# An attention and two-product kernel: blocks eight and nine share the first product, as seven products of full width

## The chip, the cores and the metric

The kernel runs on one core of one Trainium2 chip. The metric is the device time of one execution in microseconds (us). The engines are TensorE (PE for its matmuls, PEld for its weight loads), VectorE (DVE), ScalarE (ACT), GpSimd (POOL) and SyncE (SP, which here only issues DMAs).

## The reference, cut to what matters

```python
q, k, v: (8, 8, 576, 64)     # batch, heads, sequence, head width; all float32
q_s = exp(q - max(q, -1));  q_s /= sum(q_s, -1) + 1e-9
k_s = exp(k - max(k, 2));   k_s /= sum(k_s, 2) + 1e-9
kv  = einsum('bhsd,bhse->bhde', k_s, v)
x   = einsum('bhsd,bhde->bhse', q_s, kv)   # -> (4608 tokens, 512)
h   = x @ w_in                             # (4608, 512) @ (512, 2048): the first large product
g   = s * relu(h) ** 2 + b
out = g @ w_out                            # (4608, 2048) @ (2048, 512): the second large product
```

## The kernel before, in words

**Blocks and steps.** The 4608 tokens are cut into nine blocks of 512. Blocks one to eight (numbers 0 to 7 in the code) hold the first 512 tokens of each of the eight batches; block nine (number 8) holds the 64 tokens that each batch has left over. A block takes 16 steps, one for each 128 of the 2048 middle columns; step t is block t // 16, column group f = t % 16, and there are 144 steps. The weights are converted once, during block one, and stay in SBUF: `wi[f]` and `wo[f]` lie in the tile `wt[f]`.

**Three matmuls for each product.** Every operand is kept as a high and a low part (`xh`, `xl`; `w[:, 0]`, `w[:, 1]`; `gh`, `gl`) of the type float32r, and high by high, high by low and low by high are summed. So `h_parts` issues 12 matmuls of 128x512 for one step (four chunks of 128 of the 512 inputs, three matmuls each), and `o_parts` 12 more (four tiles of 128 tokens). Between them ACT makes `r = relu(h)`, DVE squares and scales it, ACT adds b and rounds it to `gh`, DVE computes `gl`. On the PE the order is h of step t, then the second product of step t - 1.

**Ahead of a block** its x is made from q, k and v (k maxima, exponentials, `kv`, `xp`), pair of heads by pair of heads. The input tiles `k0`, `q0` and `v0` are tiles of their own, filled again for each pair by SP's queue: `load_v` issues four head loads and then one for the left-over rows. The left-over 64 tokens of a pair go through a DRAM tensor, `xleft`, by `keep_left` and `store_left`; `left_over` brings all of them back as block nine's x, and ACT and POOL split it into its two parts, one chunk every second step.

**What sets the order.** Every piece of work is an `Op`: an engine, a planned cost, a due time, what it needs, takes, frees and gives. The class `Order` plays these on paper and fixes, for each engine, the order in which its instructions stand; on the chip each engine runs its own list in order and waits only for the data hazards of the tiles. The planner's costs are not times of the chip.

**The end.** The last step of block nine is cut into halves to shorten its chain, and `leave_last` copies four result tiles and stores each by two DMAs.

Of the kernel before, what the change touches and what calls it, by code (L numbers as in the profile page):

```python
# [8 lines left out]
F32 = mybir.dt.float32  # L9
F32R = mybir.dt.float32r  # L10
# [3 lines left out]
AF = mybir.ActivationFunctionType  # L14
# [12 lines left out]
def attention_moe(ctx: ExitStack, tc: tile.TileContext, q, k, v, w_in, w_out, s, b, out):  # L27
# [7 lines left out]
    NQ = 4  # L35
# [27 lines left out]
    kvfs = [const.tile([P, 2, 2, D], F32, name=f"kvf{i}") for i in range(2)]  # L63

    early = work.tile([P, 2 * NT * P], F32, name="early", tag="qhl")
    for t in kvfs:
        nc.gpsimd.memset(t, 0.0)
    sb = const.tile([P, 2], F32, name="sb")
# [7 lines left out]
    second = xpool.tile([P, 2 * NP * TB], F32, name="raw1", tag="x")  # L76
    raws = [
        (const.tile([P, KQ], F32, name="k0"), const.tile([P, KQ], F32, name="q0"), const.tile([P, VW], F32, name="v0")),
# [157 lines left out]
    def keep_left(u, x):  # L236
        pr, i = divmod(u, 2)
        if pr not in xl_:
            xl_[pr] = work.tile([P, 2, LEFT], F32, name=f"xleft_{pr}", tag="xleft", bufs=2), set()
        t, there = xl_[pr]  # L240
        nc.scalar.copy(t[:, i], x)
        there.add(i)
        if len(there) == 2 and pr < NP:
            store_left(pr)
# [207 lines left out]
    def k_tiles(pr):  # L452
        m2 = work.tile([P, 4, 2, D], F32, name=f"m2_{pr}", tag="m2")
        m1 = work.tile([P, 4, D], F32, name=f"m1_{pr}", tag="m1")
        return m2, m1, small.tile([P, 2], F32, name=f"km_{pr}", tag="km")
# [46 lines left out]
    def k_tops(pr, m):  # L502
        top = small.tile([P, 4, 2], F32, name=f"top_{pr}", tag="top", bufs=1)
# [194 lines left out]

    def left_over():

        due = NSTEP - 2 * NFC
        yield Op(
            "SP", 0.65, due, needs=[f"left{pr}" for pr in range(NP, NU // 2)] + [f"h{due - 1}"], take=["w"], kb=1024, gives=["left"]
        )
        xf = wpool.tile([P, NP, TB], F32, name="xleft_all", tag="w")
        nc.sync.dma_start(xf, xleft)
        xh, xl = x_tile(B)
        for c in range(NP):
            yield Op("ACT", 0.55, due + 2 * c, needs=["left"] + [f"h{due + 2 * c}"])
            nc.scalar.copy(xh[:, c], xf[:, c])  # L710
            yield Op("POOL", 1.1, due + 2 * c, gives=[f"x{B * NP + c}"])
            nc.gpsimd.tensor_tensor(out=xl[:, c], in0=xf[:, c], in1=xh[:, c].bitcast(F32), op=ALU.subtract)
# [25 lines left out]
    def step(t):  # L738
# [10 lines left out]
        yield Op("ACT", 0.5, t - 2, take=["r", "g"], free=["h"] if t < NSTEP - 1 else ())  # L749
        r, gh, gl = g_tiles(t)  # L750
        if t == NSTEP - 1:

            halves = [slice(i * TB // 2, (i + 1) * TB // 2) for i in range(2)]
            for i, c in enumerate(halves):
                if i:
                    yield Op("ACT", 0.35, t - 2, free=["h"])
                nc.scalar.activation(r[:, c], hp_[:, c], AF.Relu)
            for c in halves:
                yield Op("DVE", 0.4, t - 2)
                nc.vector.scalar_tensor_tensor(out=r[:, c], in0=r[:, c], scalar=s_col, in1=r[:, c], op0=ALU.mult, op1=ALU.mult)  # L760
            for c in halves:
                yield Op("ACT", 0.4, t - 2)
                nc.scalar.activation(gh[:, c], r[:, c], AF.Identity, bias=b_col)
            for i, c in enumerate(halves):
                yield Op("DVE", 0.4, t - 2, free=["r"] if i else (), gives=[f"g{t}"] if i else ())
                nc.vector.scalar_tensor_tensor(
                    out=gl[:, c], in0=r[:, c], scalar=b_col, in1=gh[:, c].bitcast(F32), op0=ALU.add, op1=ALU.subtract
                )
        else:
            nc.scalar.activation(r, hp_, AF.Relu)  # L770
        if t == NSTEP - 1:
            pass
        elif first and (t % 2):
# [19 lines left out]
        for i, j in enumerate(tile_order(t)):  # L793
# [6 lines left out]
    def tile_order(t):  # L800

        return (0, 2, 1, 3) if t == NSTEP - 1 else range(NQ)

    def o_parts(t):
# [4 lines left out]
        for j in tile_order(t):  # L809
# [22 lines left out]
    def leave_last(j):  # L832

        t = NSTEP - 1

        yield Op("DVE" if j == 2 else "ACT", 0.6, t, needs=[f"o{t} {j}"])
        if not lasts:
            lasts.append(work.tile([P, 2 * NT * P], F32, name="last", tag="qhl"))
        o = work.tile([P, DO], F32, name=f"o_{B}_{j}", tag="qe", bufs=2) if j > 1 else lasts[0][:, j * DO:(j + 1) * DO]
        (nc.vector.tensor_copy if j == 2 else nc.scalar.copy)(o, acc[B, j // 2][:, j % 2])  # L840
# [6 lines left out]
    NU = B * NP  # L847
    NBLK = B + 1
# [27 lines left out]
    def others():  # L876
# [8 lines left out]
        one = small.tile([P, 1], F32, name="one", tag="one", bufs=1)  # L885
# [43 lines left out]
    def idle(us, last):  # L929
# [7 lines left out]
        "maxima": 2, "turned": 2, "xleft": 2, "tmp": NTMP, "w": NFC + 1  # L937
# [3 lines left out]
    with tc.manual_schedule(engines={E.PE, E.DVE, E.Activation, E.Pool, E.SP}):  # L941
# [42 lines left out]
```

## Time and profile before

| | |
|---|---|
| median of 3 timed runs | 872.81 us (871.5 to 873.91) |
| profiled execution, first to last instruction | 869.5 us |
| PE busy | 851.7 us, 98% |
| DVE, ACT, POOL busy | 570.8, 416.3, 91.4 us |
| matmuls of the first product | 1728 of 128x512 |
| matmuls of the second product | 1728 of 128x512 |

The profile gives the profiled execution as a span; its own time on the device is not listed apart. The median of the runs lies 3.3 us above that span (872.81 - 869.5), which is taken for what lies around it. In the profile a row of a timeline has a start, a duration, an engine, a line of the kernel, the operation with its tiles, and a count; "[idle before <-releaser]" says how long the engine had been idle and which instruction ended that. In a row that groups instructions, the numbers after the bar are busy time and the mean duration in nanoseconds.

### The profile page before, as it was taken

The page shows a single profiled execution, that of the slowest core. Times are in us where ns is not written, and L with a number is a line of the kernel's source. Part 1 is how long each engine was busy: PE and PEld are TensorE (multiplying, and loading weights), DVE is VectorE, ACT ScalarE, POOL GpSimd, SP SyncE. Part 2 cuts the span into 40 slices and gives each one's busy share as a digit, 9 for nine tenths or more (in the row PEclk, how much of TensorE's full clock was granted, in tenths as well). Part 3 has the DMA queues.
Part 4 walks back from the last instruction along what each step waited for, and adds up shares of the span by engine and source line. Part 5 has one row for each costly group of instructions (what it writes and reads, how often), then busy time and mean ns, then how long its engine had stood idle before and what let it go on. Part 6 is the DMA issues. An engine that isn't in the chain of part 4 may idle for free.

```text
span 869.5 us, 11637 instructions
## 1 busy us (share of the span) xinstructions
PE 851.7 (98%) x4367; PEld 701.9 (81%) x4367; DVE 570.8 (66%) x916; ACT 416.3 (48%) x694; POOL 91.4 (11%) x117
## 2 busy tenths in 40 slices
PE   7799999999999999999999999999999999999997
PEld 6578887888888888888888888888888888888886
DVE  6999997596877777686677658785855322232222
ACT  5989864544554545353545354444544322222222
POOL 1000002021102111111021202020200010000000
PEclk9999999999999999999999999999999999999999
DMA  8994134424433334342433242432311000000001
GB/s 232 308 378 136 26 86 118 127 74 97 137 82 89 83 119 100 90 92 78 130 89 83 89 130 75 96 89 82 77 61 52 33 16 1 1 30 19 1 1 48
DMA packets 109991, 79.44 MB, mean 91 GB/s; under 512 B 60656, under 2 KB 103664, under 8 KB 109808
## 3 DMA queue, kind: packets, MB, share of 16 engines
q1 hardware_dynamic: 108496, 77.60, 31.8%
q10 hardware_dynamic: 1440, 1.12, 0.4%
q8 instruction: 34, 0.56, 0.3%
q14 instruction: 21, 0.17, 0.1%
HBM read 60.29 MB, written 18.40 MB: 91 GB/s over the span
## 4 chain that ended last, share of the span: by engine, by line
PE 92%; DVE 4%; DMA 1%; SPq 1%; issue 1%; ACT 0%; ACTq 0%; DVEq 0%
PE acc L814 44%; PE h L726 44%; PE kv L299 2%; PE xp L676 1%; PE xq L676 1%; DMA k<-in_k_dram 1%; DVE low L216 1%; DMA st<-in_moe_w_in_dram 0%; DVE st L213 0%; PE xp L440 0%; DVE w L223 0%; DMA v<-in_v_dram 0%; SPq L288 0%; DVE low L206 0%; DVE st L211 0%
## 5 line engine op out<-in xcount | busy, mean ns | idle before, releaser
L726 PE MATMUL h<-x,w 128*128 128x512 f32 x1728 | 420.2, 391 | 2.4 <-ACT r L770 1.2
L726 PEld LDWEIGHTS h<-x,w 128*128 128x128 f32 x1728 | 322.7, 188 | 71.6 <-ACT r L770 1.9
L814 PE MATMUL acc<-w,gh 128*128 128x512 f32 x1152 | 357.8, 392 | 0.8 <-ACT gh L780 0.8
L814 PEld LDWEIGHTS acc<-w,gh 128*128 128x128 f32 x1152 | 214.0, 188 | 45.6 <-ACT gh L780 1.2
L785 DVE SCALAR_TENSOR_TENSOR r<-r,sb 128x512 f32<-128x512 f32 x135 | 106.1, 786 | 190.1 <-ACT r L770 189.7
L814 PE MATMUL acc<-w,gl 128*128 128x512 f32 x576 | 224.5, 390 | 0.6 <-DVE gl L782 0.6
L770 ACT ACTIVATE r<-h 128x512 f32<-128x512 f32 x143 | 85.5, 598 | 277.3 <-PE h L726 264.9
L789 DVE SCALAR_TENSOR_TENSOR gl<-r,sb,gh 128x512 fp32r<-128x512 f32 x135 | 104.5, 774 | 56.5 <-ACT gh L787 55.2
L787 ACT ACTIVATE gh<-r,sb 128x512 fp32r<-128x512 f32 x135 | 97.7, 724 | 84.8 <-DVE r L785 84.4
L814 PEld LDWEIGHTS acc<-w,gl 128*128 128x128 f32 x576 | 108.1, 188 | 23.8 <-DVE gl L782 1.1
L575 POOL TENSOR_TENSOR q<-q,qm 128x640 f32<-128x640 f32 x24 | 33.7, 1406 | 161.4 <-DVE qm L573 161.4
L592 POOL TENSOR_TENSOR qe<-qe,qr 128x640 f32<-128x640 f32 x24 | 32.3, 1347 | 65.8 <-DVE qr L588 43.7
L682 ACT COPY y<-xp 64x320 f32<-64x320 f32 x48 | 20.2, 420 | 13.8 <-PE xp L676 13.4
L686 DVE TENSOR_TENSOR y<-xp,y 64x320 f32<-64x320 f32 x48 | 23.5, 489 | 3.4 <-ACT y L682 2.5
L562 ACT ACTIVATE k<-k 128x640 f32<-128x640 f32 x24 | 17.7, 737 | 15.1 <-DVE k L524 12.3
L596 DVE STREAM_TRANSPOSE q<-qe 128x640 f32<-128x640 f32 x24 | 19.9, 831 | 5.2 <-POOL qe L592 5.2
L299 PEld LDWEIGHTS kv<-v,k 128*64 128x64 f32 x600 | 18.7, 137 | 5.1 <-issue 4.4
L656 POOL TENSOR_TENSOR spare<-kvf,spare 128x256 fp32r<-128x256 f32 x12 | 10.1, 844 | 118.6 <-issue 112.8
L613 DVE TENSOR_TENSOR qhl<-qT,qhl 64x640 fp32r<-64x640 f32 x24 | 20.6, 860 | 1.1 <-ACT qhl L610 0.4
L686 DVE TENSOR_TENSOR y<-xq,y 64x256 f32<-64x256 f32 x48 | 20.3, 422 | 1.0
L299 PE MATMUL kv<-v,k 128*64 128x65 f32 (+1 forms) x600 | 20.8, 224 | 0.0
L200 ACT ACTIVATE low<-st 128x1024 int32<-128x1024 uint32 (+1 forms) x17 | 18.9, 1111 | 3.2 <-DVE w L223 1.9
(124 smaller groups left out, 619.6 us busy)
## 6 DMA issues: line engine op xcount, KB each, us to landing
st<-in_moe_w_in_dram SPq DMA_DIRECT2D x16, 512.0 KB, 8.7
st<-in_moe_w_out_dram SPq DMA_DIRECT2D x16, 512.0 KB, 9.1
out_dram<-o SPq DMA_DIRECT2D x16, 512.0 KB, 2.7
turned<-q SPq DMA_DIRECT2D x24, 320.0 KB, 2.3
qT<-turned SPq DMA_DIRECT2D x48, 160.0 KB, 3.0
k<-in_k_dram SPq DMA_DIRECT2D x14, 512.0 KB, 4.2
q<-in_q_dram SPq DMA_DIRECT2D x14, 512.0 KB, 5.3
v<-in_v_dram SPq DMA_DIRECT2D x56, 128.0 KB, 4.8
```

Of the source, the lines that this page charges most:

```text
L299: nc.tensor.matmul(kv[h * D:(h + 1) * D, i], kt[:, i, h, n], vt[:, 2 * i + h, n], start=(n == 0), stop=(n == NT - 1))
L575: nc.gpsimd.tensor_tensor(out=qt, in0=qt, in1=bc(qm, [P, 2, NT, D]), op=ALU.subtract)
L592: nc.gpsimd.tensor_tensor(out=qe_, in0=qe_, in1=qr, op=ALU.mult)
L613: nc.vector.tensor_tensor(out=t[half[1 - h], h], in0=qT[half[h]], in1=t[half[h], h].bitcast(F32), op=ALU.subtract)
L682: nc.scalar.copy(y[half[h], at], parts[h][a][half[1 - h]])
L686: nc.vector.tensor_tensor(out=y[half[h], at], in0=parts[h][a][half[h]], in1=y[half[h], at], op=ALU.add)
L726: nc.tensor.matmul(hp_, w[:, j, c, :], x[:, c, :], start=(c == 0 and i == 0), stop=(c == NP - 1 and i == 2))
L770: nc.scalar.activation(r, hp_, AF.Relu)
L785: nc.vector.scalar_tensor_tensor(out=r, in0=r, scalar=s_col, in1=r, op0=ALU.mult, op1=ALU.mult)
L787: nc.scalar.activation(gh, r, AF.Identity, bias=b_col)
L789: nc.vector.scalar_tensor_tensor(out=gl, in0=r, scalar=b_col, in1=gh.bitcast(F32), op0=ALU.add, op1=ALU.subtract)
L814: nc.tensor.matmul(acc[blk, j // 2][:, j % 2], g[:, js], w_, start=(f == 0 and i == 0), stop=(f == NFC - 1 and i == 2))
```

## The change

**The products.** Steps 112 to 143 (blocks eight and nine) are taken out of the loop of steps. For each pair p of column groups (f = 2p and 2p + 1, eight pairs) the four products of two column groups with two blocks are a two by two product of matrices: rows are the column groups, columns the blocks, and the inner dimension is split in two halves of 256. It is computed by seven products of half the depth instead of eight (a scheme of Strassen's kind, in Winograd's form). One product is 6 matmuls of 128x512. Three PSUM banks collect them: U takes products 0, 2, 4 and 5 in turn, each added onto what stands there, and ACT copies U out after 0, 2 and 4 (u1, u2, u3); A takes product 1, B takes 3 and, after a result was read, 6.

**The operands.** Sums of the weights' quarters (S1 to S4) are made by POOL for each pair, rounded by ACT, and their low parts are made by POOL again (`sums`). Sums of the two blocks' x (T1 to T4) and block nine's second half (B22) are made once by DVE, with a rounding by ACT each (`differences`, `cast`). `left_over` loads block nine's x at due time 104 and no longer splits it as it stands.

**The second product.** Block eight's pieces of it are strewn between the products of the next pair (`late_pe`). Block nine's g tiles are kept in the weight tiles `wt` that are no longer needed, and its second product comes last of all: four tiles, one after another, 48 matmuls each (`final`).

**Memory.** To make room, `k0`, `q0` and `v0` become slices of one tile, `area`; the tiles for the maxima and for the left-over tokens become slices of one tile, `misc`; some small tiles become slices of `sb`. What is loaded and in which order stays.

```diff
-    kvfs = [const.tile([P, 2, 2, D], F32, name=f"kvf{i}") for i in range(2)]
+    kvboth = const.tile([P, 2, 2, 2, D], F32, name="kvf")
+    kvfs = [kvboth[:, i] for i in range(2)]
+    area = work.tile([P, AREA], F32, name="area", tag="area")
+    misc = const.tile([P, 2, TB], F32, name="misc")
     raws = [
-        (const.tile([P, KQ], F32, name="k0"), const.tile([P, KQ], F32, name="q0"), const.tile([P, VW], F32, name="v0")),
+        (area[:, 0:KQ], area[:, KQ:2 * KQ], area[:, 2 * KQ:2 * KQ + VW]),
...
+    def cast(name, src, needs, due, gives=(), free=(), take=(), eng="DVE"):
+        yield Op("ACT", 1.04, due, needs=needs, take=take, gives=[f"{name} high"])
...
+        nc.scalar.copy(t[0], src())
+        yield Op("DVE", 1.25, due, gives=[f"{name} there"] + list(gives), free=free)
+        nc.vector.tensor_tensor(out=t[1], in0=src(), in1=t[0].bitcast(F32), op=ALU.subtract)
...
+    def sums(i):
+        f, M, odd = 2 * i, TB // 2, i % 2
...
+            w = wt[f + 1 - j][:, 0].bitcast(F32)
+            nc.gpsimd.tensor_tensor(out=F[j], in0=w[:, 0], in1=w[:, 1], op=ALU.add)
+        a21, a22, a11, a12 = (F[j][:, k * M:(k + 1) * M] for j in range(2) for k in range(2))
+        steps = (a22, a21, a22, ALU.add), (a11, a22, a11, ALU.subtract), (a12, a12, a11, ALU.subtract)
...
+        nc.scalar.copy(sh, F[1])
+        nc.gpsimd.tensor_tensor(out=sl, in0=F[1], in1=sh.bitcast(F32), op=ALU.subtract)
...
+    PROD = (
+        ("A11", "B11", "U"), ("A12", "B21", "A"), ("S2", "T2", "U"), ("S1", "T1", "B"), ("S3", "T3", "U"), ("A22", "T4", "U"), ("S4", "B22", "B")
+    )
...
+        for c in range(2):
+            for a, b_ in ((0, 0), (0, 1), (1, 0)):
+                nc.tensor.matmul(
+                    BANK[where], w(a)[:, c * P:(c + 1) * P], xs[b_][:, c], start=k in (0, 1, 3) and n == 0, stop=n == 5, skip_group_check=True
+                )
...
+    def late_pe():
+        t0 = (B - 1) * NFC
+        for p in range(HP):
+            o = (x for t in (2 * p - 2, 2 * p - 1) if p for x in pieces(t0 + t))
+            for k, n in ((0, 1), (1, 1), (3, 0), (2, 2), (4, 2), (5, 1), (6, 1)):
+                yield from product(p, k)
+                for _ in range(n):
+                    yield from next(o, ())
...
+    def quadrant(p, n):
...
+            nc.scalar.copy(row(), BANK["U"])
+            nc.vector.tensor_tensor(out=row(), in0=BANK[("A", "B", "B")[n]], in1=row(), op=ALU.add)
+            nc.scalar.activation(row(), row(), AF.Relu)
...
+    def final(j):
...
+            for i, (g, w_) in enumerate(((gh, w[:, 0]), (gh, w[:, 1]), (gl, w[:, 0]))):
+                nc.tensor.matmul(t_, g[:, js], w_, start=(f == 0 and i == 0), stop=(f == NFC - 1 and i == 2))
...
-            + [step(t) for t in range(NSTEP)]
+            + [step(t) for t in range(NSTEP - 2 * NFC)]
...
+            + operands() + [sums(i) for i in range(HP)] + [late_pe()] + [quadrant(p, n) for p in range(HP) for n in range(4)] + [final(j) for j in range(NQ)]
```

**Where instructions stand now, first place: the PE in block eight.** Before, on the PE, one step is 12 matmuls of `h` and 12 of `acc` (the second product's tiles; the numbers at a name's end count tiles):

```order
L726 MATMUL h_6229<-x_5598,w_516 128x512 x12
L814 MATMUL acc_0_6208<-w_480,gh_6213 128x512 x2
L814 MATMUL acc_0_6208<-w_480,gl_6214 128x512
L814 MATMUL acc_2_6220<-w_480,gh_6213 128x512 x2
L814 MATMUL acc_2_6220<-w_480,gl_6214 128x512
```

Now, on the PE in pair 1, products 0 and 1 (banks `q_6127`, which is U, and `qa`, which is A), 3 (`q_6144`, which is B), 2, 4, 5 and 6 follow with pieces of the second product between:

```order
L864 MATMUL q_6127<-x_100,w_511 128x512 x6
L1037 MATMUL acc_0_6230<-w_290,gh_6188 128x512 x2
L1037 MATMUL acc_0_6230<-w_290,gl_6189 128x512
L864 MATMUL qa<-x_100,w_511 128x512 x6
...
L864 MATMUL q_6144<-area_late,w_572 128x512 x6
L864 MATMUL q_6127<-area_late,set_6194 128x512
...
L1037 MATMUL acc_2_6272<-w_290,gh_6188 128x512 x2
L1037 MATMUL acc_2_6272<-w_290,gl_6189 128x512
...
L864 MATMUL q_6127<-t_6113,set_6194 128x512 x6
...
L864 MATMUL q_6127<-t_6113,w_572 128x512 x6
...
L864 MATMUL q_6144<-b_0_6062,set_6194 128x512
```

Between products 2 and 4, and between 4 and 5, which all go onto U, stand two pieces (6 matmuls) each; in pair 0 there are only four pieces in all, and one of them stands between products 4 and 5.

**Second place: ACT in block eight.** Before, ACT has two instructions for a step there, `r` from PSUM and `gh` from `r` (and once a block the copy of a result, `o`):

```order
L787 ACTIVATE gh_6668<-r_6667,sb 128x512
L770 ACTIVATE r_6699<-h_6683 128x512
L825 COPY o_0_6710<-acc_0_6208 128x1024
L787 ACTIVATE gh_6700<-r_6699,sb 128x512
L770 ACTIVATE r_6738<-h_6717 128x512
```

Now, in one of the later pairs, its queue from u1 on stands as follows; `q_6127` is the bank U, `misc` holds u2 and u3, and the CAST rows round sums of weights for the pair after:

```order
L913 COPY r_6559<-q_6127 128x512
L932 ACTIVATE w_661<-misc,sb 128x512
L917 ACTIVATE r_6559<-r_6559 128x512
L913 COPY misc<-q_6127 128x512
L932 ACTIVATE gh_6606<-r_6559,sb 128x512
L913 COPY misc<-q_6127 128x512
L799 CAST set_6194<-kvf 128x512
L917 ACTIVATE misc<-misc 128x512
L920 ACTIVATE r_6632<-q_6127 128x512
L932 ACTIVATE w_854<-misc,sb 128x512
L803 CAST w_977<-F 128x256
L932 ACTIVATE gh_6655<-r_6632,sb 128x512
```

Fourteen instructions of ACT now serve a pair, where four steps had eight, and each copy of U (the first, fourth and sixth row) stands in one queue behind roundings of other results.

**Third place: SP's queue where the third pair of heads is loaded**, with what each load waits for (`DMAHW` are semaphores of earlier DMAs). Before:

```order
L288 DMA v_92<-in_v_dram 128x4x64 [waits DMAHW0_49]
L288 DMA v_92<-in_v_dram 128x4x64 [waits DMAHW1_49]
L289 DMA v_92<-in_v_dram 64x4x64 [waits DMAHW2_49]
L184 DMA st_386<-in_moe_w_in_dram 128x4x256 [waits DMAHW3_49]
L186 DMA st_386<-in_moe_w_out_dram 128x1024 [waits DMAHW4_49]
```

Now:

```order
L291 DMA area<-in_v_dram 128x4x64 [waits DMAHW0_49]
L291 DMA area<-in_v_dram 128x4x64 [waits DMAHW1_49]
L292 DMA area<-in_v_dram 64x4x64 [waits DMAHW2_49,DMAHW7_49,DMAHW1_49,DMAHW0_49]
L187 DMA st_382<-in_moe_w_in_dram 128x4x256 [waits DMAHW3_49]
L189 DMA st_382<-in_moe_w_out_dram 128x1024 [waits DMAHW4_49]
```

The load of the left-over rows of v now waits until the head loads just ahead of it have landed, since all of them write the one tile `area`; the weight loads `st` stand behind it. The same row stands so in every later load of v.

More of the change, by code (lines that the diff above doesn't have):

```diff
@@ L697, in x_late @@
             store_left(pr)
+    xf, X8, SET, LATE = [], {}, {}, {}
     def left_over():
-        due = NSTEP - 2 * NFC
-        yield Op(
-            "SP", 0.65, due, needs=[f"left{pr}" for pr in range(NP, NU // 2)] + [f"h{due - 1}"], take=["w"], kb=1024, gives=["left"]
-        )
[L705 to L712, printed above, removed]
+        yield Op("SP", 0.65, DUE_X, needs=[f"left{pr}" for pr in range(NP, NU // 2)], take=["w"], kb=1024, gives=["left"])
+        xf.append(wpool.tile([P, NP, TB], F32, name="xleft_all", tag="w"))
+        nc.sync.dma_start(xf[0], xleft)
@@ L748, in step @@
             hp_ = next(parts)
-        yield Op("ACT", 0.5, t - 2, take=["r", "g"], free=["h"] if t < NSTEP - 1 else ())
+        yield Op("ACT", 0.5, t - 2, take=["r", "g"], free=["h"])
         r, gh, gl = g_tiles(t)
[L751 to L773, printed above, removed]
+        nc.scalar.activation(r, hp_, AF.Relu)
+        if first and (t % 2):
             yield Op("ACT", 0.67, t - 2)
```

223 lines of the change are left out of this document (204 added, 19 removed).

## The prediction

> **What bounds the kernel now.** I read the page's head and chain first, then busy time by stretch, then the timeline at three places: the steady steps, the end, and the first 60 us.
>
> ```profile
> span 869.5 us, 11637 instructions
> PE 92%; DVE 4%; DMA 1%; SPq 1%; issue 1%; ACT 0%; ACTq 0%; DVEq 0%
> 20.00:60.00 40.00, 33.16 (x182) 24.76 (x181) 38.37 (x55) 36.73 (x56) 0.12 (x1) 1.00 1.04 338
> 60.00:100.00 40.00, 40.00 (x214) 32.87 (x215) 39.83 (x55) 37.34 (x51) 0.78 (x4) 1.00 0.44 137
> 725.00:750.00 25.00, 25.00 (x112) 20.67 (x112) 6.92 (x9) 5.42 (x9) 0.51 (x1) 1.00 0.00 0
> ```
>
> The span is the profiled execution's; the median of the runs, 872.81, lies 3.3 us above it, and I keep that distance. In a row of the stretches the first number after the length is PE's busy time, then PEld's, DVE's, ACT's, POOL's, the granted clock and the DMA share. From 60 us on PE is never idle, at a clock of 1.00, and in the stretch from 725 on DVE works 28% of the time and ACT 22%. So a matmul taken out there is worth its full place in PE's queue, until another engine makes PE wait. Before 60 us the reverse holds: DVE is busy for 38.37 of 40 us, and PE waits.
>
> **What a matmul is worth, and how long a hand-over takes.**
>
> ```profile
> 671.08 2.88 PE L726 MATMUL h<-x,w 128*128 128x512 f32 x12
> 674.00 0.60 ACT L770 ACTIVATE r<-h 128x512 f32<-128x512 f32 x1 [3.29 <-PE h L726]
> 674.63 0.75 DVE L785 SCALAR_TENSOR_TENSOR r<-r,sb 128x512 f32<-128x512 f32 x1 [3.14 <-ACT r L770]
> 676.52 2.88 PE L726 MATMUL h<-x,w 128*128 128x512 f32 x12
> ```
>
> Two steps start 676.52 - 671.08 = 5.44 us apart and hold 24 matmuls: 0.227 us each. Twelve take 2.72 us of the queue, so the next could start at 673.80; ACT reads the bank at 674.00, 0.20 later, and takes 0.60. DVE follows ACT after 0.03.
>
> **Part 1, the matmuls.** Before, 32 steps of 12: 384. Now 8 pairs x 7 products x 6: 336. 48 x 0.227 = 10.9 us less, all in the stretch where PE is never idle. The second product keeps its 32 x 12 in another order, and since a product has the same three matmuls per chunk, I take the same pace.
>
> **Part 2, the end.**
>
> ```profile
> 856.06 2.88 PE L726 MATMUL h<-x,w 128*128 128x512 f32 x12
> 862.38 0.59 ACT L840 COPY last<-acc 128x512 f32<-128x512 f32 x1 [1.55 <-PE acc L814]
> 863.01 0.72 PE L814 MATMUL acc<-w,gh 128*128 128x512 f32 x2
> 864.38 0.40 PE L814 MATMUL acc<-w,gl 128*128 128x512 f32 x1
> ```
>
> From the last h to the last matmul stand 35 places: 35 x 0.227 = 7.93 us, while 864.38 - 856.06 = 8.32. The missing 0.39 us are tiles that wait for copies of a neighbour in their bank (PE at 863.01 follows ACT's end at 862.97, so that hand-over takes 0.04). `final` gives each tile a bank of its own and 48 matmuls (10.9 us) of cover, so the 0.39 goes; what follows the last matmul, one copy of 0.59 and two stores, stays. Bounds: 0 to -0.39, a little more if the last two stores, no longer crowded by six others, land sooner.
>
> **Part 3, the steady pairs (1 to 7).** A pair holds 42 + 24 matmuls, 66 x 0.227 = 14.96 us. The tight place is bank U: product 4 adds onto it only after ACT has copied product 2's result, and product 5 likewise. ACT needs 0.20 + 0.60 + 0.04 = 0.84 us; two pieces of the second product, 1.36 us, stand between. So 0.52 us to spare, if ACT is free. I followed ACT's queue with the durations here and in the next fence: u2 is due 7.0 us into a pair, and the instruction ahead of it, the relu of the first result, ends at about 5.2; u3 is due at 9.7, and the rounding ahead of it, which waits until PE has freed its buffer at 8.2, ends at 9.1. Products 6 and 0 wait for an add of DVE and a relu of ACT with 1.8 and 1.9 us to spare. ACT's 14 instructions come to at most 10 x 0.60 + 4 x 0.72 = 8.9 us of 14.96, DVE's 11 to 3 x 0.68 + 8 x 0.78 = 8.3. I take no wait: 0.
>
> ```profile
> L785 DVE SCALAR_TENSOR_TENSOR r<-r,sb 128x512 f32<-128x512 f32 x135 | 106.1, 786 | 190.1 <-ACT r L770 189.7
> L787 ACT ACTIVATE gh<-r,sb 128x512 fp32r<-128x512 f32 x135 | 97.7, 724 | 84.8 <-DVE r L785 84.4
> L449 DVE TENSOR_TENSOR x<-xp,x 128x512 fp32r<-128x512 f32 x8 | 5.5, 681 | 1.6 <-ACT xleft L241 1.4
> L656 POOL TENSOR_TENSOR spare<-kvf,spare 128x256 fp32r<-128x256 f32 x12 | 10.1, 844 | 118.6 <-issue 112.8
> ```
>
> What could spoil this is POOL, idle there before, which now has 3 instructions of 128x512 and 6 of 128x256 in each pair but the last:
>
> ```profile
> 693.04 1.23 DVE L825 COPY o<-acc 128x1024 f32<-128x1024 f32 x1 [1.34 <-PE acc L814]
> 693.90 1.29 POOL L712 TENSOR_TENSOR x<-xleft_all,x 128x512 fp32r<-128x512 f32 x1 [46.23 <-ACT x L710]
> 694.18 1.56 DVE L789 SCALAR_TENSOR_TENSOR gl<-r,sb,gh 128x512 fp32r<-128x512 f32 x1
> ...
> 698.00 0.76 DVE L789 SCALAR_TENSOR_TENSOR gl<-r,sb,gh 128x512 fp32r<-128x512 f32 x1 [0.79 <-ACT gh L787]
> ...
> 702.40 1.35 POOL L712 TENSOR_TENSOR x<-xleft_all,x 128x512 fp32r<-128x512 f32 x1 [7.21 <-ACT x L710]
> 703.39 0.91 DVE L789 SCALAR_TENSOR_TENSOR gl<-r,sb,gh 128x512 fp32r<-128x512 f32 x1 [0.79 <-ACT gh L787]
> ```
>
> A DVE instruction of 0.76 us that meets POOL takes 1.56 or 0.91, and both times it ends 0.55 us after POOL does (695.74 against 695.19, 704.30 against 703.75): of its 0.76 us, 0.55 can't run beside POOL. The copy from PSUM at 693.04 kept its usual length with POOL beside it. So per pair the shared path carries 3 x 1.32 + 6 x 0.84 = 9.0 us of POOL and 8 x 0.55 = 4.4 of DVE (the three adds read PSUM): 13.4 of 14.96. It fits; each meeting delays DVE by up to 1.3 us, and the slacks of 1.8 us and more absorb one. Bounds for the seven pairs: 0 to the price of the port rival below.
>
> The Trainium skill (SBUF — State Buffer, "Who interferes with whom") says that a DVE instruction with two SBUF inputs and a GpSimd one that reads SBUF exclude each other for the whole instruction. By that rule the path carries 9.0 + 8 x 0.76 = 15.1 us, above 14.96, for 7 pairs: 1 us more on the sum. The trace agrees on the exclusion and has 0.55 instead of 0.76 for its length.
>
> **Part 4, pair 0.** Product 0 starts where step 112's h stood.
>
> ```profile
> 667.48 0.34 SPq L706 DMA_DIRECT2D xleft_all<-xleft  x1
> xleft_all<-xleft SPq DMA_DIRECT2D x1, 1024.0 KB, 4.8
> 687.40 2.88 PE L726 MATMUL h<-x,w 128*128 128x512 f32 x12
> L223 DVE TENSOR_TENSOR w<-low,w 128x1024 fp32r<-128x1024 f32 x15 | 18.3, 1222 | 0.3 <-ACT w L221 0.3
> ```
>
> Block nine's x lands at 672.3, 15 us ahead. In that time DVE has seven of its eleven 128x1024 instructions (1.22 each) between the steps' own work, and ends the parts for products 3, 2 and 4 about 2.5 us before, 1.5 after and 0.4 after product 0's start, when they are wanted at 2.7, 4.8 and 7.5. The fourth set needs block seven's x to be out of use: its rounding on ACT stands behind the copy of a result and ahead of u3, so u3 ends near 10.1 us, while product 5 could start at 9.5. I take +0.65 us. Bounds: 0 if ACT gets there sooner, +3 if two more 128x1024 instructions are late.
>
> **Part 5, the loads.** One tile `area` makes the last load of v wait for the head loads.
>
> ```profile
> L288 SPq DMA_DIRECT2D v<-in_v_dram x4: 571/1480/2736, 30.7 to 35.8; - x4
> v<-in_v_dram SPq DMA_DIRECT2D x2, 128.0 KB, 4.9
> 37.17 0.63 SPq L289 DMA_DIRECT2D v<-in_v_dram  x1
> 38.49 0.50 SPq L186 DMA_DIRECT2D st<-in_moe_w_out_dram  x1
> st<-in_moe_w_out_dram SPq DMA_DIRECT2D x1, 512.0 KB, 5.6
> 44.24 1.18 ACT L200 ACTIVATE low<-st 128x1024 int32<-128x1024 uint32 x1
> 46.52 0.60 ACT L770 ACTIVATE r<-h 128x512 f32<-128x512 f32 x1 [1.09 <-PE h L726]
> 59.92 0.50 PE L814 MATMUL acc<-w,gl 128*128 128x512 f32 x1 [0.64 <-DVE gl L782]
> ```
>
> The last head load starts at 35.8 and lands about 4.9 later (the last two's median), near 40.5, so SP's next load goes out about 3 us after 37.17, and the weights behind it too. They landed at 38.49 + 5.6 = 44.1; ACT took them at 44.24, without a gap. With the DMA engines emptier, I put the landing 2.5 us later: ACT's idle 1.09 covers part, and some 1.2 us stay in its queue, which has no gap until 58 us, and about 1.0 of it reaches PE at 59.92, where PE already waits for DVE. After 60 us PE has no idle time to catch up with: +1.0 us. Bounds: 0 to +3. The later loads of v have over 8 us before SP's next load and cost nothing.
>
> **Sum.** -10.9 - 0.4 + 0 + 0.65 + 1.0 = -9.6 us: a span of 859.9, and 863.2 with the 3.3 around it.
>
> **Rivals.**
> *U hand-over.* If another ACT instruction (0.72) is in front of u2 or u3, a hand-over takes 1.56 against 1.36: 0.2 x 14 = 2.8 us, 866.0; with two in front 0.92 x 14 = 12.9. For it: one queue for fourteen instructions. Against: the slacks of Part 3.
> *Port full.* The exclusion lasts for the whole DVE instruction and queueing comes on top: 1 to 3 us, 864 to 866. That is the rule named above. For it: 13.4 of 14.96 is little room.
> *Operands late.* Pair 0 and the loads both cost their bounds, 3 + 3 instead of 1.65: 867.6. For it: the trace shows no wait like them.
> *DVE and POOL never overlap, the adds from PSUM included: slower.* A pair then takes 9.0 + 8.3 = 17.3 us, 2.3 above PE's, in seven pairs: +16, 879. Slower begins where a pair takes 14.96 + 9.6 / 7 = 16.3. Against: the copy at 693.04.
>
> **How the numbers follow.** Chances: forecast 0.60, U 0.12, port 0.10, operands 0.10, slower 0.08 (half of that within the band). The measurement tells about 0.3% (2.6 us). Faster means under 870.2: the first four cases less a rest, 0.87; same 0.07; slower 0.06. Bounds added from below: no costs of Parts 4 and 5 and 0.5 us gained at the stores, 861; from above the operands' 867.6 and a little waiting on U: 868.5.
>
> **What would show it.** In the changed profile: 48 matmuls fewer; PE without idle from pair 1 on, a gap of about half a microsecond ahead of product 5 in pair 0; SP's weight loads near 41 us; PE's last wait in the first stage near 61 instead of 59.9; DVE instructions of 1.3 us and more beside POOL without a wait of PE. Idle time of PE in every pair would make the prediction wrong, by U if ACT releases it, by the port if DVE does.

## The result, and the profile after

| | before | after |
|---|---|---|
| median of the runs, us | 873.0 (871.5 to 873.91, 4 runs) | 865.13 (864.44 to 865.89, 4 runs) |
| profiled execution: time, span, us | span 869.5 | 864.44, span 862.6 |
| mean granted clock in it | 1.000 | 0.997 |

The ratio is 0.9916 (95% interval 0.9902 to 0.993): 7.9 us less by the medians of four runs each, 6.9 by the two spans. Two later sets of runs, with more runs of the kernel before, have 872.14 to 865.06 and 871.95 to 865.0, 7.1 and 7.0 us less, so the spans tell the gain better here. The forecast was 9.6 less and 863.2 us; the time lies 1.9 us above it, inside its bounds of 861 and 868.5.

The page of the changed kernel, head and chain, and its busy time by stretch (after the length come PE, PEld, DVE, ACT, POOL, each with its count, then the granted clock, the DMA share and GB/s):

```profile
span 862.6 us, 11740 instructions
PE 90%; DMA 3%; SPq 2%; DVE 2%; issue 1%; ACT 1%; ACTq 0%
675.00:700.00 25.00, 24.59 (x109) 20.06 (x108) 20.58 (x21) 13.60 (x19) 4.82 (x6) 1.00 0.05 22
700.00:725.00 25.00, 23.80 (x104) 18.93 (x103) 20.50 (x22) 13.44 (x24) 17.59 (x15) 1.00 0.05 22
725.00:750.00 25.00, 25.00 (x111) 20.61 (x110) 15.46 (x19) 13.91 (x25) 14.83 (x15) 1.00 0.00 1
```

PE still sets the time. From 725 us on it has no idle, while DVE's work in that stretch rose from 6.92 to 15.46 us, ACT's from 5.42 to 13.91 and POOL's from 0.51 to 14.83. Between 675 and 725 us PE now misses 0.41 and 1.20 us. The timeline of PE shows where: the first rows below are the first product of pairs 0, 1, 2, 3 and 7, the next three are PE's only idle times in the pairs (start, length, then in brackets the idle time and its releaser).

```profile
688.76 1.52 PE L864 MATMUL q<-x,w 128*128 128x512 f32 x6
701.76 1.55 PE L864 MATMUL q<-x,w 128*128 128x512 f32 x6
718.62 1.52 PE L864 MATMUL q<-x,w 128*128 128x512 f32 x6
733.67 1.55 PE L864 MATMUL q<-x,w 128*128 128x512 f32 x6
793.86 1.55 PE L864 MATMUL q<-x,w 128*128 128x512 f32 x6
698.92 1.63 PE L864 MATMUL q<-t,w 128*128 128x512 f32 x6 [0.41 <-ACT misc L913]
707.98 0.50 PE L864 MATMUL q<-area_late,set 128*128 128x512 f32 x1 [0.57 <-ACT r L913]
711.62 1.65 PE L864 MATMUL q<-t,set 128*128 128x512 f32 x6 [0.63 <-ACT misc L913]
```

Pair 0 takes 13.00 us, pair 1 takes 16.86, and pairs 2 to 6 take (793.86 - 718.62) / 5 = 15.05 each. The 698.92 row is product 5 of pair 0; 707.98 is product 2 and 711.62 product 4 of pair 1. All three wait for L913, ACT's copy of bank U. A wait costs more than the listed idle time. From the start of the matmul ahead to the start of the one that waited are 0.802, 0.955 and 1.017 us instead of 0.227, and from there to the next one 0.33 to 0.34: 0.68, 0.84 and 0.90 us lost for 0.41, 0.57 and 0.63 listed.

At the start of the kernel and at its end:

```profile
37.97 4.52 PE L974 MATMUL h<-x,w 128*128 128x512 f32 x12 [1.00 <-ACT r L999]
40.05 0.62 SPq L292 DMA_DIRECT2D area<-in_v_dram  x1
41.36 0.50 SPq L189 DMA_DIRECT2D st<-in_moe_w_out_dram  x1
47.12 1.18 ACT L203 ACTIVATE low<-st 128x1024 int32<-128x1024 uint32 x1 [1.82 <-DMA st<-in_moe_w_out_dram]
61.22 0.50 PE L1037 MATMUL acc<-w,gl 128*128 128x512 f32 x1 [0.63 <-DVE gl L1009]
845.62 12.40 PE L960 MATMUL last<-w 128*128 128x512 f32 x54
858.05 0.58 ACT L1063 COPY last<-last 128x512 f32<-128x512 f32 x1 [21.17 <-PE last L960]
```

SP's load of v's left-over rows went out at 40.05 instead of 37.17, the weights behind it 2.9 us later, ACT waited 1.82 us for them, and PE's last wait of the first stage ended at 61.22 instead of 59.92. But the twelve matmuls at 37.97 took 4.52 us instead of 3.06, before the late load could act, so this profile has two candidates for that shift. At the end no tile waits: 54 matmuls start one after another (53 x 0.22665 and the last one's 0.39 come to the row's 12.40 us).

With 0.22665 us a matmul (the steady steps of before: 265 intervals, mean 0.2266) the two profiles are accounted for:

| part | forecast, us | measured, us | from |
|---|---|---|---|
| 48 matmuls less | -10.9 | -10.9 | 48 x 0.22665 |
| start, up to product 0 | +1.0 | +1.36 | 688.76 - 687.40 |
| pair 0 | +0.65 | +0.76 | 13.00 - 54 x 0.22665 |
| pair 1 | 0 | +1.90 | 16.86 - 66 x 0.22665 |
| pairs 2 to 7 and after | 0 | +0.5 | 5 x 0.09, and 0.08 from 793.86 on |
| end: copies between tiles, and the tail | -0.4 | -0.56 | -0.42 of waits, 5.10 to 4.96 behind the last matmul |
| sum | -9.6 | -6.9 | span 869.48 to 862.59 |

### The profile page after: what moved, and what is told of

The parts are those of the page before. It is cut to its first block, busy times and chain, and to the rows that moved or that the text cites. A ratio compares the mean times of both kernels' runs of the same rounds, so it can differ in the third digit from the quotient of the medians.

```text
span 862.6 us, 11740 instructions
## 1 busy us (share of the span) xinstructions
PE 844.3 (98%) x4319; PEld 694.7 (81%) x4319; DVE 613.0 (71%) x949; ACT 440.8 (51%) x741; POOL 166.1 (19%) x184
## 4 chain that ended last, share of the span: by engine, by line
PE 90%; DMA 3%; SPq 2%; DVE 2%; issue 1%; ACT 1%; ACTq 0%
PE acc L1037 39%; PE h L974 34%; PE q L864 7%; PE last L960 5%; PE kv L302 2%; DMA st<-in_moe_w_out_dram 1%; PE qa L864 1%; PE xp L679 1%; PE xq L679 1%; DMA area<-in_k_dram 1%; SPq L282 1%; SPq L291 1%; DMA area<-in_v_dram 0%; PE xp L443 0%; SPq L275 0%
## 5 line engine op out<-in xcount | busy, mean ns | idle before, releaser
L974 PE MATMUL h<-x,w 128*128 128x512 f32 x1344 | 329.4, 392 | 2.2 <-ACT r L999 1.2
L1037 PE MATMUL acc<-w,gh 128*128 128x512 f32 x1024 | 318.2, 392 | 0.8 <-ACT gh L1007 0.8
L974 PEld LDWEIGHTS h<-x,w 128*128 128x128 f32 x1344 | 251.8, 189 | 56.7 <-ACT r L999 1.9
L1037 PEld LDWEIGHTS acc<-w,gh 128*128 128x128 f32 x1024 | 190.1, 188 | 40.3 <-ACT gh L1007 1.2
L1037 PE MATMUL acc<-w,gl 128*128 128x512 f32 x512 | 199.6, 390 | 0.6 <-DVE gl L1009 0.6
L1012 DVE SCALAR_TENSOR_TENSOR r<-r,sb 128x512 f32<-128x512 f32 x104 | 83.6, 804 | 89.5 <-ACT r L999 89.1
L1014 ACT ACTIVATE gh<-r,sb 128x512 fp32r<-128x512 f32 x104 | 75.2, 723 | 63.3 <-DVE r L1012 62.9
L578 POOL TENSOR_TENSOR area<-area,qm 128x640 f32<-128x640 f32 x24 | 33.1, 1381 | 162.8 <-DVE qm L576 162.8
L960 PE MATMUL last<-w 128*128 128x512 f32 x192 | 43.7, 389 | 0.0
L960 PEld LDWEIGHTS last<-w 128*128 128x128 f32 x192 | 36.0, 188 | 7.5
L934 DVE SCALAR_TENSOR_TENSOR gl<-r,sb,gh 128x512 fp32r<-128x512 f32 x16 | 13.8, 860 | 17.1 <-ACT gh L932 17.1
```

Of the source, the lines that this page charges most:

```text
L578: nc.gpsimd.tensor_tensor(out=qt, in0=qt, in1=bc(qm, [P, 2, NT, D]), op=ALU.subtract)
L960: nc.tensor.matmul(t_, g[:, js], w_, start=(f == 0 and i == 0), stop=(f == NFC - 1 and i == 2))
L974: nc.tensor.matmul(hp_, w[:, j, c, :], x[:, c, :], start=(c == 0 and i == 0), stop=(c == NP - 1 and i == 2))
L1012: nc.vector.scalar_tensor_tensor(out=r, in0=r, scalar=s_col, in1=r, op0=ALU.mult, op1=ALU.mult)
L1014: nc.scalar.activation(gh, r, AF.Identity, bias=b_col)
L1037: nc.tensor.matmul(acc[blk, j // 2][:, j % 2], g[:, js], w_, start=(f == 0 and i == 0), stop=(f == NFC - 1 and i == 2))
```

## The experiments

The theories: **A**, the late load of v causes the loss at the start; **B**, the slow matmuls at 38 us cause it. **P**, POOL's sums stretch DVE's instructions (an instruction takes longer while one of POOL's runs beside it) and so cause pair 1's waits; **Q**, DVE's and ACT's own queues are late there. Ratios are to runs of the kernel before on the same chip, with their 95% intervals.

### again and v_last: the start

*again* is the changed kernel itself.

> The changed kernel once more, as the control for the others. What can move by itself is the clock: in its first profile the granted clock was at half for 3.41 us from about 38 us on, and the twelve matmuls of the h at 37.97 took 4.52 us instead of 3.06. If that is a matter of where a window of the clock falls, some runs do not show it. Theory A (the late weight load sets the start, the slow matmuls are hidden behind it): product 0 of pair 0 starts near 688.8 with or without the half clock. Theory B (the half clock is the start's loss): without it, product 0 starts near 687.5 and the time is 1.3 us less. The three waits for copies of bank U in pairs 0 and 1 should come again: 0.41, 0.57 and 0.63 us in the first profile.

*v_last*, cut to the place that sets the order (`pr == NP // 2` is the third pair of heads; there `load_v` issues the four head loads and `load_v_left` the left-over rows):

```diff
-            yield Op("SP", 3.2, due, needs=[f"kv{p}"], gives=[f"v{pr} there"], kb=1100)
-            load_v(pr)
+            if pr != NP // 2:
...
+            else:
+                yield Op("SP", 2.6, due, needs=[f"kv{p}"], gives=[f"v{pr} main"], kb=1100)
+                load_v(pr)
+                yield Op("SP", 0.6, VL, needs=[f"v{pr} main", "w6 1 there"], gives=[f"v{pr} there"], kb=64)
+                load_v_left(pr)
```

> Only the load of v's left-over rows for the third pair of heads is moved: behind the weights' loads up to f=8, so that its wait for the four head loads holds up no weights. Nothing else changes its place. Theory A: SP's load of weight f=5 goes out near 37.2 instead of 40.7, ACT takes it near 44.2 instead of 47.1, PE's last wait in the first stage ends near 60.0 instead of 61.2, and the time is 1.3 us less than the control's (864). Theory B (the half clock): with the half clock in the profile PE's last wait still ends near 61.2; without it both kernels gain alike, and the load is worth nothing. Half a microsecond or less of gain would speak for B.

Measured: again 865.06 (864.8 to 865.72), ratio 0.9921 (0.9906 to 0.9936); v_last 864.13 (863.41 to 865.02), ratio 0.9911 (0.9894 to 0.9927). The times overlap, so the traces have to decide. Before, first and last row of the stretch in question (the last, 59.92, stands in the prediction), then the same places of again, then of v_last:

```profile
36.24 0.72 PE L726 MATMUL h<-x,w 128*128 128x512 f32 x2 [0.33 <-DVE x L449]
```

```profile
36.97 0.73 PE L974 MATMUL h<-x,w 128*128 128x512 f32 x2 [0.34 <-DVE x L452]
41.46 0.60 SPq L187 DMA_DIRECT2D st<-in_moe_w_in_dram  x1
47.61 1.17 ACT L203 ACTIVATE low<-st 128x1024 int32<-128x1024 uint32 x1 [2.55 <-DMA st<-in_moe_w_out_dram]
61.73 0.50 PE L1037 MATMUL acc<-w,gl 128*128 128x512 f32 x1 [0.64 <-DVE gl L1009]
```

```profile
36.92 0.73 PE L979 MATMUL h<-x,w 128*128 128x512 f32 x2 [0.33 <-DVE x L457]
37.48 0.62 SPq L187 DMA_DIRECT2D st<-in_moe_w_in_dram  x1
44.93 1.16 ACT L203 ACTIVATE low<-st 128x1024 int32<-128x1024 uint32 x1
60.60 0.50 PE L1042 MATMUL acc<-w,gl 128*128 128x512 f32 x1 [0.65 <-DVE gl L1014]
```

From the first row to the last are 59.92 - 36.24 = 23.68 us before, 24.76 in again, 23.68 in v_last. Neither of the last two has the slow matmuls at 38 us, so the load by itself costs 1.08 us, and moving it brings all of that back: A holds. The slow matmuls add nothing that stands out. In the first profile, which has them, the stretch is 61.22 - 36.24 = 24.98 us. Of the ten profiles of kernels with the late load, the four with slow matmuls at 38 us have 24.89 to 24.98 and the six without have 24.63 to 24.96. So the load costs 0.95 to 1.3 us, 1.2 on average, with slow matmuls or without. Product 0 of pair 0 says the same: in the three of these profiles with no half clock before the end (pool_more, piece and leave_both, told of below) it starts at 688.62, 688.72 and 688.86, near the 688.8 of theory A, while B expected 687.5.

What slows these matmuls is the clock. Busy time of PE, granted clock, DMA share and GB/s, in the first profile of the changed kernel around 38 us, and in again around 17 us:

```profile
34.41:37.83 3.42, 1.59 (x5) 1.00 1.14 225
37.83:41.24 3.41, 3.27 (x8) 0.50 0.28 52
```

```profile
13.33:16.74 3.41, 1.26 (x11) 1.00 1.24 247
16.74:20.15 3.41, 3.41 (x46) 0.50 1.23 251
```

For 3.41 us the clock is at half, right behind a window of the same length in which PE was busy for 46% (1.59 of 3.42 us) or 37% (1.26 of 3.41). In the other profiles that window has 43 to 57%. But two windows of the first profile in which PE was busy for 52 and 53% (from 13.94 and from 31.00 us) were not followed by half clock, so these runs don't show where the line lies. In the thirteen profiles after the prediction the half clock came near 38 us four times, near 17 six times, and not at all before the end three times, in kernels whose instructions for the first 36 us are alike.

### no_pool, pool_more, pool_memset: what POOL does

*no_pool*:

```diff
-                nc.gpsimd.tensor_tensor(out=a21, in0=a11, in1=a21, op=ALU.subtract)
+                if i < 2: nc.gpsimd.tensor_tensor(out=a21, in0=a11, in1=a21, op=ALU.subtract)
...
```

and so for all of POOL's instructions in `sums`. The instructions of the other engines stay.

> POOL's instructions of the weight sums are left out from the third pair's sums on (its sums and its low halves, nine instructions a pair), so the sums of pairs 2 to 7 are wrong values; PE, ACT and DVE have the same instructions as in the changed kernel. POOL's last instruction is then near 705 us. Theory P (POOL stretches DVE, which hands U's buffers on late): the two waits of pair 1, which cost 1.8 us with the restart of PE behind them, are gone, pair 0's stays (0.7), and if the pace of 15.05 us a pair also comes from POOL's traffic the pairs go back to 14.96, 0.5 more: 1.8 to 2.3 us below the control. Rival Q (DVE and ACT are late in pairs 0 and 1 by their own queues): the waits of pair 1 stay at 1.2 us and the time is that of the control within 0.5.

Measured: 862.79 (862.51 to 863.4), ratio 0.9895 (0.988 to 0.9909), 2.3 us under again. The waits of pair 1 are gone: pair 1 takes 717.30 - 702.25 = 15.05 us. But pairs 2 and 3 take 15.06 and 15.03, so the 0.09 us a pair above 66 x 0.22665 do not come from POOL. How POOL made the waits is seen side by side, first in the changed kernel, then in no_pool (gl L934 of pair 0 frees the buffer r; w L934 frees the buffer u2):

```profile
705.09 1.61 POOL L780 TENSOR_TENSOR F<-w 128x512 f32<-128x512 f32 x1
705.48 1.77 DVE L934 SCALAR_TENSOR_TENSOR gl<-r,sb,gh 128x512 fp32r<-128x512 f32 x1
707.34 0.58 ACT L913 COPY r<-q 128x512 f32<-128x512 f32 x1 [1.79 <-DVE gl L934]
709.72 1.17 DVE L934 SCALAR_TENSOR_TENSOR w<-misc,sb,w 128x512 fp32r<-128x512 f32 x1 [0.19 <-ACT w L932]
710.98 0.58 ACT L913 COPY misc<-q 128x512 f32<-128x512 f32 x1 [0.77 <-DVE w L934]
```

```profile
705.96 0.74 DVE L934 SCALAR_TENSOR_TENSOR gl<-r,sb,gh 128x512 fp32r<-128x512 f32 x1
708.15 0.75 DVE L934 SCALAR_TENSOR_TENSOR w<-misc,sb,w 128x512 fp32r<-128x512 f32 x1
```

PE waited for ACT, ACT for the buffer, and the buffer for DVE instructions of 1.77 and 1.17 us instead of 0.75.

*pool_more*:

```diff
-            nc.gpsimd.tensor_tensor(out=F[j], in0=w[:, 0], in1=w[:, 1], op=ALU.add)
+            for _ in range(2 if i > 1 else 1):
+                nc.gpsimd.tensor_tensor(out=F[j], in0=w[:, 0], in1=w[:, 1], op=ALU.add)
```

> The two sums of weight chunks of 128x512 that POOL makes for a pair are made twice, from the third pair's on: two more POOL instructions of 1.32 us in six pairs, 2.64 us a pair, same values. By the row of the prediction (0.55 us of a DVE instruction with two SBUF inputs cannot run beside POOL) the shared path then carries 13.4 + 2.6 = 16.0 us against PE's 15.0: 1.0 us in six pairs, about 6 us slower than the control, with DVE releasing the waits. If the exclusion holds for the whole DVE instruction it carries 17.7: 16 us slower. If POOL and DVE hardly exclude each other, POOL is busy 11.6 of 15 us and nothing changes.

Measured: 870.23 (869.25 to 871.48), ratio 0.998 (0.997 to 0.9989), 5.2 us over again. That is close to the 6 of my row, and the 16 of whole-instruction exclusion are out. But the trace does not tell the story of the row. Two pair starts of pool_more, ACT's waits from 733 to 780 us (us in all, times, longest), and POOL's doubled sums of one pair with the instruction behind them:

```profile
750.20 1.65 PE L865 MATMUL q<-x,w 128*128 128x512 f32 x6 [0.46 <-ACT r L921]
766.66 1.66 PE L865 MATMUL q<-x,w 128*128 128x512 f32 x6 [0.47 <-ACT r L921]
ACT set L800 <- POOL kvf L789: 7.0, 2, 3.5
755.40 3.00 POOL L781 TENSOR_TENSOR F<-w 128x512 f32<-128x512 f32 x2
761.30 1.19 POOL L789 TENSOR_TENSOR F<-F 128x256 f32<-128x256 f32 x1
```

A pair takes 16.46 us, and in each ACT stands 3.5 us in its queue before a sum's rounding that waits for POOL's last sum; the relu that frees bank U stands behind that rounding. The changed kernel's list for the same stretch has no such wait. So the last run put other work of the same length into POOL.

*pool_memset*:

```diff
+            for _ in range((3, 2)[j] if i > 1 else 0):
+                nc.gpsimd.memset(F[j], 0.0)
             nc.gpsimd.tensor_tensor(out=F[j], in0=w[:, 0], in1=w[:, 1], op=ALU.add)
```

> In place of the doubled sums of pool_more, POOL fills the two 128x512 buffers of the sums with zeros, five times 0.53 us a pair = 2.6 us, ahead of the sums, in the same six pairs; the values stay the same. It tells apart why pool_more was 5 us slower, where the trace showed ACT 3.5 us a pair in its queue behind a rounding that waits for POOL's last sum. Port theory: what lengthens a pair is that DVE's instructions cannot run beside POOL's sums; a fill has no input to read from SBUF, so DVE is not stretched by it and the pairs stay at 15.05 or gain 0.2: the control's 865 to 866.5. Chain theory: POOL's sums come 2.6 us later, ACT's queue waits for them and PE for ACT, whatever POOL does in that time: 16.2 to 16.5 us a pair, 870 as in pool_more.

Measured: 866.32 (866.12 to 866.86), ratio 0.9934 (0.9918 to 0.9951).

```profile
747.85 1.64 PE L866 MATMUL q<-x,w 128*128 128x512 f32 x6 [0.64 <-ACT r L922]
763.84 1.66 PE L866 MATMUL q<-x,w 128*128 128x512 f32 x6 [0.66 <-ACT r L922]
ACT set L801 <- POOL kvf L790: 11.5, 3, 3.8
753.02 1.69 POOL L781 MEMSET F<- 128x512 f32 x3
758.47 1.19 POOL L790 TENSOR_TENSOR F<-F 128x256 f32<-128x256 f32 x1
753.15 0.75 DVE L936 SCALAR_TENSOR_TENSOR w<-misc,sb,w 128x512 fp32r<-128x512 f32 x1 [0.79 <-ACT w L934]
```

By its time alone this would speak for the port; its trace speaks for the chain. A pair takes 15.99 us with the same wait of ACT for POOL's last sum, though DVE beside the fill keeps its 0.75 us. So of pool_more's 1.41 us a pair above 15.05, 0.94 come with fills too. The other 0.47 lie in POOL's chain as well: from the first of the added instructions to the one behind the sums POOL needs 761.30 - 755.40 = 5.90 us in pool_more and 758.47 - 753.02 = 5.45 here, 0.45 less. The sums of pool_more take 1.5 us each where they run beside DVE's instructions, those here 1.28 to 1.30. So what is left fits POOL's own sums being stretched, and a delay of DVE is not needed to explain it. The total is small because pair 1 gained: its sums came later, past DVE's crowded microseconds, and it took 716.93 - 701.90 = 15.03 us, without its waits.

### leave_dve, leave_both, piece: the queues of pairs 0 and 1

*leave_dve* (in `leave`, for the block before the pair of blocks; *leave_both* has `"u3 0"` in place of `"T4 high"`):

```diff
-        yield Op(eng, (0.98, 1.18)[j], t - 2, needs=[f"o{t} {2 * j}", f"o{t} {2 * j + 1}"], take=["tmp"], free=["acc"])
+        yield Op(eng, (0.98, 1.18)[j], t - 2, needs=[f"o{t} {2 * j}", f"o{t} {2 * j + 1}"]
+                 + ["T4 high", f"g{t + 2}"][j:j + 1] * (blk == B - 2), take=["tmp"], free=["acc"])
```

> The two copies by which the block before leaves PSUM are moved: DVE's (1.21 us) from ahead of the c12 add of pair 0 to behind the last rounding of pair 0, ACT's (1.01 us) from ahead of the rounding of T4 to just behind it; in DVE's queue one add also changes places with a rounding. Rival Q (DVE's queue is late in pair 1 because of its own work): the instruction that frees the buffer r in pair 1 ends 1.2 us sooner, so the wait of 0.57 ahead of product 2 goes, and with its restart 0.9 us; the wait ahead of product 4 behind it stays or grows by what the first let through. Theory P (POOL's sums stretch DVE): DVE's instruction is stretched by POOL all the same, and the gain is under 0.5. Pair 0's wait stays 0.4, since as much ACT work stands ahead of its copy as before.

> As leave_dve, but ACT's copy of the block before goes behind the third copy of bank U in pair 0. By the step of the prediction on pair 0, T4's rounding then starts near 695.7 instead of 696.7, its low half is there near 698.0 instead of 699.0, and the copy of U goes out as soon as product 4 has ended: the wait ahead of product 5 falls from 0.41 to 0.2 or less, 0.4 us with the restart, on top of what leave_dve gains. The order of ACT's queue in the later pairs moves too (sums' roundings ahead of copies of U): if two ACT instructions in front of a copy cost what the U rival of the prediction says, new waits of 0.2 to 0.9 us stand in pairs 2 to 6 and eat the gain.

*piece*:

```diff
-            for k, n in ((0, 1), (1, 1), (3, 0), (2, 2), (4, 2), (5, 1), (6, 1)):
+            for k, n in ((0, 1), (1, 1), (3, p == 1), (2, 2 + (p == 1)), (4, 2), (5, p != 1), (6, p != 1)):
```

> In pair 1 alone the pieces of the second product stand otherwise: one more ahead of product 2, one more between products 2 and 4, none behind products 5 and 6. PE reaches product 2 of pair 1 0.68 us later and product 4 1.36 later, with work instead of waits: the waits of 0.57 and 0.63 us go, 1.8 us with their restarts, if products 6 and 0 behind still find DVE's add and ACT's relu done (slacks 1.9 and 1.8 us by the prediction less 0.7 and 0.7). If these come late instead, the waits move to product 6 of pair 1 or product 0 of pair 2, and the time is the control's. ACT's order moves in the later pairs too, as in leave_both.

Measured: leave_dve 862.62 (862.43 to 862.85), ratio 0.989 (0.9875 to 0.9905); leave_both 862.64 (862.51 to 863.14), ratio 0.9891 (0.9875 to 0.9908); piece 863.65 (863.38 to 864.79), ratio 0.9904 (0.9889 to 0.9919). Of leave_dve the starts of pairs 1 and 2, the one wait left, the instruction that frees r, and DVE's last instruction for T4, which waits for ACT's rounding; the last row is that instruction in the changed kernel:

```profile
701.53 1.55 PE L864 MATMUL q<-x,w 128*128 128x512 f32 x6
716.56 1.52 PE L864 MATMUL q<-x,w 128*128 128x512 f32 x6
698.65 1.65 PE L864 MATMUL q<-t,w 128*128 128x512 f32 x6 [0.21 <-ACT misc L913]
703.00 1.23 DVE L934 SCALAR_TENSOR_TENSOR gl<-r,sb,gh 128x512 fp32r<-128x512 f32 x1
696.62 1.23 DVE L720 TENSOR_TENSOR t<-xleft_all,t 128x1024 fp32r<-128x1024 f32 x1 [1.48 <-ACT t L718]
```

```profile
697.80 1.23 DVE L720 TENSOR_TENSOR t<-xleft_all,t 128x1024 fp32r<-128x1024 f32 x1 [2.60 <-ACT t L718]
```

Pair 1 takes 15.03 us, both of its waits gone, though POOL still stretches gl to 1.23 us: it starts 2.5 us sooner. I had expected only the first wait to go, and pair 0's to stay at 0.41; it fell to 0.21. The 2.5 us come from both moves. DVE's instruction for T4 starts 1.2 us sooner, since ACT's copy of the block before no longer stands ahead of T4's rounding, and DVE's own copy of 1.21 us is out of the way. Whether one of the two would have been enough was not run. So P and Q are both halves of the cause: DVE's queue was late without POOL's doing, and POOL stretched what was late; with either taken away (no_pool, leave_dve) pair 1 has no wait. In pool_memset, where the sums come later, it has none either. leave_both leaves no wait in pairs 0 and 1 that the list shows, though 0.27 us are lost ahead of product 5 of pair 0, and 0.26 us are lost in pair 4, where ACT's order had moved; it is no better. piece traded pair 1's 1.74 us for 0.41 of short waits there and 0.32 in pair 3.

### eight: what the matmuls are worth

```diff
+        for again in range(1 + (k == 1)):
             ...                              # product 1's six matmuls
```

> Product 1 of each pair is issued twice over (the second time from its first matmul with start, so the values stay the same): 48 matmuls more, as many as the change removed, everything else in place. If a matmul is worth its full place in PE's queue the stretch gets 48 x 0.227 = 10.9 us longer; but product 2 of pair 1 and product 5 of pair 0 come 1.36 us later, which is more than the 0.4 to 0.6 us that they wait for ACT's copies, so the waits of pairs 0 and 1 (2.5 us with the restarts of PE) should go: a net 8.4 us above the control, 873.5. With the waits unchanged it would be 876. If the pairs were bound by DVE or POOL and not by PE, less than 5 us would be added.

Measured: 874.66 (874.13 to 876.28), ratio 1.0033 (1.0022 to 1.0044): 9.6 us over the changed kernel's 865.06. One pair as a stretch, columns as above:

```profile
753.42:769.83 16.41, 16.41 (x73) 13.52 (x72) 9.09 (x12) 8.03 (x15) 9.80 (x10) 1.00 0.00 0
```

A pair is 16.41 - 15.05 = 1.36 us longer, which is six full places (6 x 0.227). Of the waits only those of pair 1 shrank, from 1.74 to 0.43 us lost; pair 0's stayed at 0.41 listed, which I had wrong. 8 x 1.36 - 1.3 = 9.6.

### control, both_moves, both_moves_u3

> The changed kernel beside the two combinations, on their chip: 864.5 to 865.5 us, 0.992 of the kernel before.

> v_last and leave_dve in one kernel. The first takes 1.0 us out of the start, the second 2.4 us out of pairs 0 and 1, at places 600 us apart, so the gains should add: 3.4 us below the control, 861.6, and PE without any wait after 62 us but for 0.2 ahead of product 5 of pair 0. If PE's start in pair 0 had been what made pair 1 late, the second gain would shrink.

> v_last and leave_both in one kernel: pair 0 without a wait, but 0.3 us lost in pair 4, as leave_both showed alone: the same 861.6 within 0.3 us.

Measured: control 865.0 (864.45 to 865.66), ratio 0.9918 (0.9903 to 0.9933); both_moves 862.1 (861.41 to 862.38), ratio 0.9883 (0.9866 to 0.9899); both_moves_u3 862.21 (861.74 to 862.47), ratio 0.9885 (0.9871 to 0.99). All executions of both are below all of the control's: 2.9 us less, instead of 3.4. From product 0 to pair 2 both_moves takes 27.86 us against the control's 29.87, 2.01 less, and the stretch of the start that v_last was judged by is 23.66 against 24.63, 0.97 less: 2.98 in all. Most of the 0.5 that I missed is leave_dve's, which I had put at 2.4 from the times of two chips; inside the trace it is 2.0. With both_moves_u3, which the times don't tell from it, this is the fastest version here, 1.2% below the kernel before.

## Why the prediction was right, and where it was off

The gain came as forecast from 48 matmuls that each are worth a full place, and the losses of the start and of pair 0 came where they were expected. A loss of 1.9 us in pair 1 and a slightly slower pace, 0.5 us in all, were not expected, and a wrong allowance around the span happened to cover half of what was missed.

- **Matmuls, -10.9.** Right: eight put six places a pair back at 1.36 us.
- **The end, -0.39.** Right: 0.42 us of waits gone, and 0.14 behind the last matmul.
- **Loads, +1.0.** Right in cause and nearly in size: 1.08 between again and v_last, 0.95 to 1.3 over the ten profiles. The half clock at 38 us, which the sum did not have, added nothing that stands out.
- **Pair 0, +0.65.** Right in place (ahead of product 5), in cause and nearly in size: 0.68 for the wait, 0.76 in all. When ACT's copy went behind T4's rounding (leave_dve), the wait halved.
- **Steady pairs, 0.** The failed step is the sentence "each meeting delays DVE by up to 1.3 us, and the slacks of 1.8 us and more absorb one". Pair 1 is not steady: DVE came into it late from pair 0's operands and the two copies of the block before, and there meetings of 1.0 and 0.4 us reached PE, 1.74 us in two waits. I had counted the queues of a steady pair and used the result for pair 1. The releaser was the U hand-over, as in that rival, but behind buffers that DVE freed late, not behind two ACT instructions.
- **Steady pace.** Pairs 2 to 6 are 0.09 us longer than 66 full places. no_pool and eight have the same, so POOL does not make it, and six more matmuls in a pair do not change it. In before's steady steps all 265 intervals are 0.226 or 0.227 us; in the pairs some 60 of 263 are 0.229 to 0.238, in clusters. Why stays open.
- **The port, 13.4 of 14.96.** In the steady pairs it cost nothing, as forecast: pairs take the same with POOL (15.05 us) and without (15.03 to 15.06). But pool_more and pool_memset show that it was not the path that binds when POOL gets more work. POOL's own chain through ACT's roundings is: with 2.6 us more in POOL, ACT waits for POOL's last sum whether or not DVE is hindered. I had not counted that chain. The page SBUF — State Buffer of the Trainium skill ("Who interferes with whom") says that a DVE instruction with two SBUF inputs contends with a GpSimd instruction that reads SBUF, not with one that only writes it. The trace agrees: 0.75 us beside a fill, 1.77 beside a sum.
- **The 3.3 us around the span.** Wrong: each execution's time is 1.75 to 1.93 above its own span (864.44 and 862.6 in the first profile). I had subtracted the span of one execution from the median of others. That error of 1.4 us and the 2.7 us by which the sum overrated the gain have opposite signs, so by luck the forecast is closer than its steps were.
- **PE never idle from 60 us on.** Nearly: the profile before has one wait of PE between 62 and 856 us, 0.20 us at 131.91, and the changed kernel has it too (133.24).

## What to carry to other kernels

Slack counted in a steady loop holds in the steady loop; its first rounds, in which the queues still carry the work of the stage before, need a count of their own, and here moving two copies of 1.0 and 1.2 us there was worth 2.0 us. When two streams of loads come to share a tile, look at what stands in the queue behind the one that now waits. And compare a time with the span of the same execution, never with that of another.

## What the runs showed of the hardware

- The clock fell to half for 3.41 us behind stretches of the same length in which PE was busy for 37 to 57%, without having been idle throughout, while other stretches with 52 and 53% did not bring it. Where it came changed from one execution to the next: near 17 us, near 38 us or not before the end. The Trainium skill (TensorE: Matmul & The Clock Gate, "What's actually happening") says that a free-running window of 3413 ns decides, and that the same kernel varies with its phase. The trace agrees on the length and the variation; the page has the half rate follow an idle window, and here half-busy ones sufficed.
- A wait of PE listed as 0.57 us cost 0.84: the matmul that waited started 0.955 us after the one ahead of it, 0.16 more than the usual 0.227 and the wait together, and the next one followed after 0.34 instead of 0.227.
- A DVE instruction of 0.75 us with two inputs in SBUF took up to 1.77 beside a sum of POOL and 0.75 beside a fill. POOL's sum of 128x512 was stretched too: 1.29 to 1.75 us in the changed kernel's first profile.
